# Linear attention and spectral mixing: k and v loaded in 18-row runs, and the first output tile finished whole

## The chip, the core and the metric

The kernel runs on one core of one Trainium2 chip. The metric is the device time of one execution in microseconds (us). The kernel before was timed three times: 426.86, 425.69 and 426.14 us, a median of 426.14 us. The core's engines are TensorE (PE in the profile; PEld is its weight load), VectorE (DVE), ScalarE (ACT), GpSimd (POOL) and SyncE (SP). In this kernel POOL and SP issue all transfers, which 16 DMA engines carry out.

## What is computed

A linear attention with feature map elu(x)+1 over 8 batches, 8 heads, 576 rows and 64 columns, then a spectral mix over the rows:

```python
q_p, k_p = phi(q), phi(k)
kv  = einsum('bhsd,bhse->bhde', k_p, v);  z = sum(k_p, axis=2)
x   = einsum('bhsd,bhde->bhse', q_p, kv) / (einsum('bhsd,bhd->bhs', q_p, z)[..., None] + 1e-06)
X   = rfft(x as (B, S, 512), axis=1)[:, :64]
Y   = per mode m:  X[:, m] @ (w_r[m] + 1j * w_i[m])
u   = x + irfft(Y, n=576)
out = u + maximum(u @ w_ch, 0)
```

The inputs are float32: q, k and v of 9.4 MB each, w_r and w_i of 67 MB each. The output is 9.4 MB.

## The kernel before

**Attention stage (lines 143 to 411).** For each of the 8 batches `load(b)` brings q, k and v into SBUF as 16-bit numbers; POOL issues these loads (batch 0's q comes through SP in float32). A batch is 8 heads of 576 rows, laid one after the other. For q a partition holds 18 rows in one run (`j=2 * NJ`), two runs per partition, each run covering a pair of four-head blocks; for k and v it holds 9 rows, four runs per partition. A run is one descriptor: 4,608 bytes read and 2,304 written for q, half of that for k and v. Buffers are double (`bufs=2`), so the load of batch b+2 waits until batch b's copy has been used. `exps` (ACT) and `features` (DVE) form phi of q and k; the last DVE step of `features`, line 232, copies v into the padded tile `vpad`, of which there is one, with a column of ones. `turn_q` transposes q on PE (line 242), ACT copies the result (line 249). `sum_kv` (lines 254 to 278) multiplies phi(k) by v on PE: 36 products over 64 partitions each, alternating between the lower and the upper half of the array, then two ACT copies of 64x260 into `kv`. `form_x` (five per batch) multiplies q by kv on PE (line 165) and divides on DVE (lines 296 and 299); `transform` and `place_x` are the Fourier products. All steps are pinned: each engine runs them in the order in which the program writes them. Three PSUM tiles with the tag `big` rotate among `qTp`, `kvp`, `num` and `xp`.

**Mode stage (lines 413 to 511 and 883 to 893).** Every pair of modes needs 2 MB of weights in SBUF, loaded by POOL in two halves (line 119). Five pairs are fetched ahead during the attention stage, then the channel weights `wch` and the small constant `pick_sb`; all go through the same queue, in issue order. The pair after those five (p = 5) uses the buffer of pair 0, so its loads are issued when the products of pair 0 (line 442) are done, and those come last in the attention stage's order on PE.

**Tail (lines 896 to 989).** When the last mode's weights are in, its result `Y` is transposed and multiplied by `wch` in two column halves, `zl` and `z1l` (line 924), copied into `last`, and added to each output tile through small products (line 736), rectified (ACT, lines 785 and 965), added to x (DVE, lines 969 and 809) and stored by SP. The first output tile is treated on its own (lines 910 to 952): its second column half has PSUM of its own, `z0h1`, formed from three products (lines 913, 915 and 941); PE forms `y0l` and two of these between the two halves of line 924; then each half is added (line 942), rectified (line 943) and stored (line 950), 128 KB each. The PSUM of `zl`, `z1l`, `y0l` and `z0h1` is released before `channels(2)`, the first user of the next pool (line 775). SP issues in this order: the copy of `last` to `YZ_all` (line 954), the stores of tile 0, then those of the other tiles; POOL issues the second half of the copy to `YZ_all`.

Of the kernel before, what the change touches and what calls it, by code (L numbers as in the profile page):

```python
# [10 lines left out]
F32 = mybir.dt.float32  # L11
# [3 lines left out]
ALU = mybir.AluOpType  # L15
# [28 lines left out]
def kernel(  # L44
# [97 lines left out]

    vp = sA.tile([128, NHP, NJ, 66], F16, name="vpad")
    nc.vector.memset(vp[:, :, :, 64:66], 1.0)
# [33 lines left out]
    def load(b):  # L178
        for nm, src in (("q", q), ("k", k), ("v", v)):
            rows_in = src[b].rearrange("h s d -> (h s) d").rearrange(  # L180
                "(hp r j) d -> r hp (j d)", r=128, j=2 * NJ if nm == "q" else NJ
            )
            if (nm, b) == ("q", 0):
                for c in range(2):
                    t = sA.tile([128, 2, NJ * Dh], F32, tag="x16", bufs=2, name=f"q32_{c}")
                    pin(nc.sync.dma_start(out=t, in_=rows_in[:, :, c * NJ * Dh : (c + 1) * NJ * Dh]))
                    raw[nm, b, c] = t
                pin(nc.sync.dma_start(out=id16, in_=id16_dr.ap()))
                pin(nc.sync.dma_start(out=fwd_sb, in_=fwd_dr.ap()))
                continue  # L190
            shape = [128, 2, 2 * NJ * Dh] if nm == "q" else [128, NHP, NJ * Dh]
            t = sA.tile(shape, F16, tag=f"{nm}16", bufs=2, name=f"{nm}16_{b}")
            pin(nc.gpsimd.dma_start(out=t, in_=rows_in))
            raw[nm, b] = t

    def heads(nm, b, c):
        if (nm, b) == ("q", 0):
            return raw[nm, b, c].rearrange("p o (j d) -> p o j d", d=Dh)
        if nm == "q":
            return raw[nm, b].rearrange("p o (c j d) -> p c o j d", c=2, d=Dh)[:, c]  # L200
        return raw[nm, b].rearrange("p (o c) (j d) -> p c o j d", o=2, d=Dh)[:, c]

# [51 lines left out]
    def sum_kv(b):  # L254

        kv_ps = psA.tile([128, 2, 512], F32, tag="big", bufs=3, name=f"kvp{b}")
        for hpp in range(2):
            for j in range(NJ):
                for h2 in range(2):
                    pin(  # L260
                        nc.tensor.matmul(
                            kv_ps[:, h2, hpp * 130 : hpp * 130 + 130],
                            phi["k", b][HALVES[h2], hpp, j].rearrange("p o d -> p (o d)"),
                            vp[HALVES[h2], hpp::2, j, 0:65],
                            start=(j == 0),
                            stop=(j == NJ - 1),
                        )
                    )
# [643 lines left out]
    def second_half_sums():  # L912
        pin(nc.tensor.matmul(z0, id16, e0_parts(0)[0][1][:, COLS[1]], start=True, stop=False))
        pin(
            nc.tensor.matmul(
                z0, inv2_sb[0 : 2 * NF, rows_of(0)], YZ[0][0 : 2 * NF, 1, COLS[1]],
                start=False, stop=False,
            )
        )

    for h in range(2):
# [7 lines left out]
        pin(nc.scalar.copy(out=last[:, 1, COLS[h]], in_=last_ps[h][:, 0:hw]))  # L929
        if h == 0:  # L930
            pin(nc.tensor.matmul(y0, lead_sb[0][:, rows_of(0)], last[:, 0, :]))
            second_half_sums()
    for h in range(2):
        x = x_of(0)[:, COLS[h]]
        l, r = lead_sb[0][:, rows_of(0)], last[:, 1, COLS[h]]
        if h == 0:
            z = accs[0][:, 0, COLS[0]]
            on_bank(0, {0}, nc.tensor.matmul(z, l, r, start=False, stop=True, skip_group_check=True))
        else:
            z = z0  # L940
            pin(nc.tensor.matmul(z, l, r, start=False, stop=True))
        pin(nc.vector.tensor_tensor(out=x, in0=y0[:, COLS[h]], in1=x, op=ALU.add))
        ins = nc.vector.scalar_tensor_tensor(
            out=x, in0=z, scalar=0.0, in1=x, op0=ALU.max, op1=ALU.add
        )
        if h == 0:
            on_bank(0, {0}, ins)
        else:
            pin(ins)
        nc.sync.dma_start(  # L950
            out=out_rows[0:512, COLS[h]].rearrange("(r j) d -> r j d", j=NJJ)[:, 0, :], in_=x
        )
    for h, eng in enumerate((nc.sync, nc.gpsimd)):
# [17 lines left out]

    add_inverse(0, 1, (1,))
    relu(0, 1)
# [47 lines left out]
```

## Time and profile before

The profiled execution took 426.86 us; its span from the first to the last instruction is 425.0 us, so 1.86 us lie around it.

| what | value |
|---|---|
| profiled execution / its span | 426.86 us / 425.0 us |
| median of three executions | 426.14 us |
| busy share of the span: PE, DVE, ACT, POOL | 66%, 51%, 38%, 13% |
| DMA: moved, mean rate | 93.20 MB, 219 GB/s |
| share of the chain that ended last: DMA, PE, DVE, ACT | 63%, 21%, 5%, 4% |
| k and v loads: 16 of 576 KB, median from issue to landing | 12.8 and 14.9 us |
| weight loads: 62 of 1024 KB, median from issue to landing | 12.4 and 17.0 us |

The rate counts bytes as written; loads that narrow float32 to 16 bits read twice as many. A DMA share of 1 in a stretch means that the 16 engines' packet times add up to the stretch; it can be above 1, as packets overlap on an engine.

### The profile page before, as it was taken

The numbers are of one execution on the slowest core, as the hardware profiler recorded it, in microseconds if no ns is written. First come the engines' busy times: TensorE is split into PE (matmuls) and PEld (weight loads), VectorE is DVE, ScalarE is ACT, GpSimd is POOL, SyncE is SP. The second block draws the span as 40 slices with busy tenths as digits, with TensorE's granted clock in tenths as the row PEclk, the third lists the DMA queues.
The fourth block names the chain that finished last, engine by engine and source line by source line (L and its number), as shares of the span: only waits on it lengthen the run. The fifth ranks groups of instructions, "written<-read, shape, count | busy, mean of one in ns | idle before, by whom it ended". The sixth has DMA issues, their size and how long they took to land.

```text
span 425.0 us, 7990 instructions
## 1 busy us (share of the span) xinstructions
PE 278.9 (66%) x3429; PEld 152.0 (36%) x3429; DVE 215.6 (51%) x448; ACT 161.5 (38%) x253; POOL 56.3 (13%) x99
## 2 busy tenths in 40 slices
PE   1358378878516644434344777988887698989991
PEld 0246367666302322212122333433343333455320
DVE  4599488886203453455444443443453323513893
ACT  4688487754202102000000243443443341421781
POOL 4222124210000100000000011100000000120000
PEclk9999886889955555555555597898999986999996
DMA  9999999999999999999999999999999999994796
GB/s 213 210 208 215 207 218 204 226 210 213 225 211 220 221 216 210 216 222 216 209 217 222 214 211 216 222 215 213 217 217 218 216 214 214 219 209 87 270 395 275
DMA packets 20659, 93.20 MB, mean 219 GB/s; under 512 B 2064, under 2 KB 11408, under 8 KB 16208
## 3 DMA queue, kind: packets, MB, share of 16 engines
q0 software_dynamic: 16512, 81.47, 93.5%
q1 hardware_dynamic: 4112, 11.22, 7.1%
q8 instruction: 27, 0.44, 0.4%
q14 instruction: 8, 0.07, 0.0%
HBM read 163.93 MB, written 9.44 MB: 408 GB/s over the span
## 4 chain that ended last, share of the span: by engine, by line
DMA 63%; PE 21%; DVE 5%; ACT 4%; issue 2%; POOL 2%; DVEq 0%; POOLq 0%; ACTq 0%
DMA w<-in_moe_w_i_dram 48%; DMA pick_sb<-row_pick 8%; PE P L442 8%; DMA k<-in_k_dram 7%; PE acc L736 3%; PE acc L775 2%; PE zl L425 2%; ACT ke L213 2%; POOL w L119 1%; PE eps L677 1%; ACT qT L249 1%; DVE ys L452 1%; PE z L699 1%; PE yt L460 1%; DVE x L299 1%
## 5 line engine op out<-in xcount | busy, mean ns | idle before, releaser
L442 PE MATMUL P<-w,xt_c 64*32 64x512 bf16 (+2 forms) x1000 | 50.6, 536 | 60.3 <-DMA w<-in_moe_w_i_dram 58.9
L452 DVE CAST ys<-P 128x512 f16<-128x512 f32 x32 | 22.1, 692 | 124.2 <-PE P L442 124.2
L454 ACT CAST ys<-P 128x512 f16<-128x512 f32 x31 | 18.1, 585 | 156.1 <-PE P L442 156.1
L119 POOL DMA_DIRECT2D w<-in_moe_w_r_dram x31 | 16.4, 528 | 245.7 <-PE P L442 87.5
L442 PEld LDWEIGHTS <-xt_c 64*32 64x32 bf16 (+2 forms) x1000 | 16.6, 128 | 80.2 <-DMA w<-in_moe_w_i_dram 46.8
L165 PEld LDWEIGHTS <-qT 64*128 64x128 f16 (+1 forms) x640 | 23.0, 123 | 50.1 <-issue 30.9
L677 PE MATMUL eps<-wch,xTw 128*128 128x512 f16 x144 | 40.0, 405 | 0.0
L165 PE MATMUL num<-kv,qT 64*128 64x65 f16 (+1 forms) x320 | 13.6, 209 | 25.6 <-ACT xt_c L350 12.3
L658 DVE TENSOR_TENSOR x_main<-ya,x_main 128x512 f32<-128x512 f32 x32 | 22.0, 689 | 15.2 <-PE ya L654 15.1
L660 ACT CAST x16w<-x_main 128x512 f16<-128x512 f32 x32 | 19.8, 618 | 23.5 <-DVE x_main L658 22.5
L165 PE MATMUL nw<-kv,qT 64*128 64x65 f16 (+1 forms) x320 | 19.0, 240 | 9.5 <-DVE x_tail L621 4.3
L685 ACT CAST E<-eps 128x512 f16<-128x512 f32 (+1 forms) x40 | 21.2, 539 | 8.8 <-PE eps L677 8.8
L460 PE MATMUL yt<-pick_sb,ys 128*128 128x16 f16 x252 | 11.7, 174 | 17.7 <-DMA pick_sb<-row_pick 11.0
L299 DVE TENSOR_TENSOR x<-num,rd 128x512 f16<-128x512 f32 x32 | 22.1, 692 | 1.1
L242 PE MATMUL qTp<-id,qe 128*128 128x128 f16 x144 | 15.7, 296 | 10.1 <-DVE qe L226 9.6
L213 ACT ACTIVATE qe<-q 128x1152 f16<-128x1152 f16 (+1 forms) x16 | 17.8, 1156 | 11.0 <-DMA q<-in_q_dram 6.8
L249 ACT COPY qT<-qTp 128x1152 f16<-128x1152 f16 x16 | 19.6, 1295 | 0.5 <-PE qTp L242 0.2
L213 ACT ACTIVATE ke<-k 128x1152 f16<-128x1152 f16 x16 | 17.7, 1152 | 4.8 <-DMA k<-in_k_dram 4.8
L460 PEld LDWEIGHTS <-ys 128*128 128x128 f16 x252 | 9.7, 101 | 27.6 <-DVE ys L452 14.6
L425 PE MATMUL zl<-wch,id 128*128 128x512 f16 x72 | 19.3, 404 | 0.0
L785 ACT ACTIVATE acc<-acc 128x512 f32<-128x512 f32 x34 | 18.2, 580 | 2.4 <-PE acc L736 1.5
L242 PEld LDWEIGHTS <-qe 128*128 128x128 f16 x144 | 13.5, 137 | 11.1 <-DVE qe L226 9.9
(122 smaller groups left out, 468.3 us busy)
## 6 DMA issues: line engine op xcount, KB each, us to landing
w<-in_moe_w_r_dram POOLq DMA_DIRECT2D x31, 1024.0 KB, 12.4
w<-in_moe_w_i_dram POOLq DMA_DIRECT2D x31, 1024.0 KB, 17.0
out_dram<-x_main SPq DMA_DIRECT2D x10, 512.0 KB, 3.8
k<-in_k_dram POOLq DMA_DIRECT2D x8, 576.0 KB, 12.8
v<-in_v_dram POOLq DMA_DIRECT2D x8, 576.0 KB, 14.9
q<-in_q_dram POOLq DMA_DIRECT2D x7, 576.0 KB, 12.8
out_dram<-x_main SPq DMA_DIRECT2D x2, 1024.0 KB, 5.8
q<-in_q_dram SPq DMA_DIRECT2D x2, 576.0 KB, 4.5
```

Of the source, the lines that this page charges most:

```text
L165: mm = nc.tensor.matmul(num[hpo][orow, c0 : c0 + 65], qT[rows, hpp, h2, cols], kv_sb[rows, hpp, h2, :])
L213: pin(nc.scalar.activation(out=ev[:, c], in_=heads(nm, b, c), func=AF.Exp))
L242: nc.tensor.transpose(qT_ps[:, j], phi["q", b][:, c, j].rearrange("p o d -> p (o d)"), id16,)
L249: nc.scalar.copy(out=qT[:, :, c * NJ : (c + 1) * NJ], in_=qT_ps.rearrange("p j x -> p x j"))
L299: nc.vector.tensor_tensor(out=dst.rearrange("p (o c d) -> p o c d", o=2, c=4), in0=nv[:, :, :, 0:64], in1=rden.unsqueeze(3).broadcast_to([ ...
L425: pin(nc.tensor.matmul(last_ps[0], id16, wch16[:, 0, :]))
L442: nc.tensor.matmul(P[c : c + n, :], xt_cols(dc, kk, n), w[rows, dc, :], start=(dc < NDC), stop=(dc >= n_dc - NDC), tile_position=(rows.sta ...
L452: pin(nc.vector.tensor_copy(out=st, in_=P))
L460: nc.tensor.matmul(yt_ps[:, ec, kk % 8, :], st[:, ec * 128 : ec * 128 + 128], pick_sb)
L658: pin(nc.vector.tensor_tensor(out=x, in0=acc, in1=x, op=ALU.add))
L677: nc.tensor.matmul(e_ps, xT[:, c, :], wch16[:, c, :], start=(c == 0), stop=(c == NDC - 1))
L685: pin(nc.scalar.copy(out=dst, in_=e_ps[:, cols]))
```

## The change

Two things are done. First, k and v are loaded like q, in runs of 18 rows, two per partition. Partitions 0 to 63 of a run block then hold other heads than before, each head lying in 32 partitions, so `sum_kv` forms the products in four groups of 32 partitions: two passes (`pair`), each with its own PSUM tile, 36 products and two ACT copies of 64x130 (two heads of 65 columns). Products per batch go from 36 over 64 rows to 72 over 32 rows, copies from two to four, `big` tiles by one more per batch. Second, the first output tile is no longer split: its two halves of line 924 follow each other, `y0l` comes after them, tile 0's rectified part is accumulated whole in the PSUM pair it shares with tile 1, and it is added, rectified and stored whole (256 KB). The list `QUADS`, which decides what is stored in runs of 8 KB, stands in both kernels as `(5, 6)`.

```diff
-    vp = sA.tile([128, NHP, NJ, 66], F16, name="vpad")
+    vp = sA.tile([128, 2, 2 * NJ, 66], F16, name="vpad")
...
-                "(hp r j) d -> r hp (j d)", r=128, j=2 * NJ if nm == "q" else NJ
+                "(hp r j) d -> r hp (j d)", r=128, j=2 * NJ
...
-        kv_ps = psA.tile([128, 2, 512], F32, tag="big", bufs=3, name=f"kvp{b}")
-        for hpp in range(2):
-            for j in range(NJ):
+        for pair in range(2):
+            kv_ps = psA.tile([128, 2, 512], F32, tag="big", bufs=3, name=f"kvp{b}_{pair}")
+            for j in range(2 * NJ):
                 for h2 in range(2):
+                    r0 = 64 * pair + 32 * h2
                     pin(
                         nc.tensor.matmul(
-                            kv_ps[:, h2, hpp * 130 : hpp * 130 + 130],
-                            phi["k", b][HALVES[h2], hpp, j].rearrange("p o d -> p (o d)"),
-                            vp[HALVES[h2], hpp::2, j, 0:65],
+                            kv_ps[:, h2, 0:130],
+                            phi["k", b][r0 : r0 + 32, j // NJ, j % NJ].rearrange("p o d -> p (o d)"),
+                            vp[r0 : r0 + 32, :, j, 0:65],
...
+                            tile_position=(r0, 0),
...
-        for hpo in range(2):
-            rows = HALVES[hpo]
-            pin(
-                nc.scalar.copy(
-                    out=kv_all[b][rows],
-                    in_=kv_ps[rows, :, 0:260].rearrange("p t (c o n) -> p c t o n", c=2, o=2)[
-                        :, :, :, hpo, :
-                    ],
-                )
-            )
+            for hpo in range(2):
+                rows = HALVES[hpo]
+                pin(
+                    nc.scalar.copy(
+                        out=kv_all[b][rows, pair], in_=kv_ps[rows, :, hpo * 65 : hpo * 65 + 65]
+                    )
+                )
...
-    z0 = psW.tile([128, D], F32, tag="P", bufs=2, name="z0h1")[:, COLS[1]]
...
-        if h == 0:
-            pin(nc.tensor.matmul(y0, lead_sb[0][:, rows_of(0)], last[:, 0, :]))
-            second_half_sums()
-    for h in range(2):
-        x = x_of(0)[:, COLS[h]]
...
-        nc.sync.dma_start(
-            out=out_rows[0:512, COLS[h]].rearrange("(r j) d -> r j d", j=NJJ)[:, 0, :], in_=x
-        )
+    pin(nc.tensor.matmul(y0, lead_sb[0][:, rows_of(0)], last[:, 0, :]))
+    pin(nc.vector.tensor_tensor(out=x_of(0), in0=y0, in1=x_of(0), op=ALU.add))
...
-    add_inverse(0, 1, (1,))
+    add_inverse(0, 1)
+    on_bank(
+        0, {0},
+        nc.vector.scalar_tensor_tensor(
+            out=x_of(0), in0=accs[0][:, 0], scalar=0.0, in1=x_of(0), op0=ALU.max, op1=ALU.add
+        ),
+    )
+    store(0, 1)
     relu(0, 1)
```

More of the change, by code (lines that the diff above doesn't have):

```diff
@@ L190, in load @@
                 continue
-            shape = [128, 2, 2 * NJ * Dh] if nm == "q" else [128, NHP, NJ * Dh]
-            t = sA.tile(shape, F16, tag=f"{nm}16", bufs=2, name=f"{nm}16_{b}")
+            t = sA.tile([128, 2, 2 * NJ * Dh], F16, tag=f"{nm}16", bufs=2, name=f"{nm}16_{b}")
             pin(nc.gpsimd.dma_start(out=t, in_=rows_in))
@@ L198, in heads @@
             return raw[nm, b, c].rearrange("p o (j d) -> p o j d", d=Dh)
-        if nm == "q":
-            return raw[nm, b].rearrange("p o (c j d) -> p c o j d", c=2, d=Dh)[:, c]
-        return raw[nm, b].rearrange("p (o c) (j d) -> p c o j d", o=2, d=Dh)[:, c]
+        return raw[nm, b].rearrange("p o (c j d) -> p c o j d", c=2, d=Dh)[:, c]
     def flat(nm, b):
@@ L254, in sum_kv @@
     def sum_kv(b):
[L256 to L258 removed]
+        for pair in range(2):
+            kv_ps = psA.tile([128, 2, 512], F32, tag="big", bufs=3, name=f"kvp{b}_{pair}")
+            for j in range(2 * NJ):
                 for h2 in range(2):
+                    r0 = 64 * pair + 32 * h2
                     pin(
                         nc.tensor.matmul(
[L262 to L264 removed]
+                            kv_ps[:, h2, 0:130],
+                            phi["k", b][r0 : r0 + 32, j // NJ, j % NJ].rearrange("p o d -> p (o d)"),
+                            vp[r0 : r0 + 32, :, j, 0:65],
                             start=(j == 0),
[L266 to L276 removed]
+                            stop=(j == 2 * NJ - 1),
+                            tile_position=(r0, 0),
+                        )
+                    )
+            for hpo in range(2):
[4 more added lines that the diff above has]
+                    )
                 )
[L278 removed]
     def form_x(b, jj):
@@ L909 @@
     pin(nc.vector.tensor_copy(out=last[:, 0, COLS[1]], in_=y_ps[1].rearrange("p c r -> p (c r)")))
-    z0 = psW.tile([128, D], F32, tag="P", bufs=2, name="z0h1")[:, COLS[1]]
[L912 to L917, printed above, removed]
-            )
-        )
     for h in range(2):
@@ L929 @@
         pin(nc.scalar.copy(out=last[:, 1, COLS[h]], in_=last_ps[h][:, 0:hw]))
-        if h == 0:
-            pin(nc.tensor.matmul(y0, lead_sb[0][:, rows_of(0)], last[:, 0, :]))
-            second_half_sums()
-    for h in range(2):
-        x = x_of(0)[:, COLS[h]]
[L935 to L949, printed above, removed]
-        nc.sync.dma_start(
-            out=out_rows[0:512, COLS[h]].rearrange("(r j) d -> r j d", j=NJJ)[:, 0, :], in_=x
-        )
+    pin(nc.tensor.matmul(y0, lead_sb[0][:, rows_of(0)], last[:, 0, :]))
+    pin(nc.vector.tensor_tensor(out=x_of(0), in0=y0, in1=x_of(0), op=ALU.add))
     for h, eng in enumerate((nc.sync, nc.gpsimd)):
```

## The prediction

> **What bounds the kernel now.** I read the chain of waits first, then the rate and DMA share of stretches, then the order of single instructions where the change touches it. The chain of waits (start, length, what):
>
> ```profile
> 33.47 15.89 DMA k<-in_k_dram
> ...
> 71.94 20.44 DMA w<-in_moe_w_i_dram
> 92.66 32.88 DMA pick_sb<-row_pick
> ...
> 362.68 17.84 DMA w<-in_moe_w_i_dram
> 380.56 1.84 PE P L442 x27
> ...
> 416.63 1.13 DVEq L1016
> ```
>
> One DMA wait hands over to the next from 33 to 380 us: the time is what the queue of loads takes, as long as it never runs dry. The first and the last load of that queue are fixed, so a byte that is moved faster anywhere in it is a gain at the end. After 380.56 a chain of short PE and DVE steps follows, and then the stores. The second view is the table of stretches (stretch, length, PE, PEld, DVE, ACT, POOL busy, granted clock, DMA share, GB/s). Which load is in flight I took from the issue order of the queue and the lengths of the loads; the first two stretches hold k and v only, the next two mostly q, the last weights only:
>
> ```profile
> 45.60:50.20 4.60, 0.31 (x4) 0.21 (x2) 1.61 (x5) 2.97 (x3) 0.00 (x0) 0.95 1.21 208
> 67.80:72.00 4.20, 3.55 (x74) 3.04 (x68) 3.38 (x8) 3.59 (x6) 2.76 (x5) 0.72 1.20 206
> ...
> 51.30:53.20 1.90, 0.88 (x12) 0.63 (x11) 0.38 (x2) 0.94 (x2) 0.00 (x0) 0.50 1.12 213
> 73.40:75.00 1.60, 0.19 (x2) 0.16 (x2) 1.39 (x3) 1.58 (x3) 0.70 (x2) 1.00 1.12 214
> 280.00:320.00 40.00, 32.00 (x303) 14.57 (x301) 16.71 (x32) 16.61 (x31) 4.23 (x8) 0.96 1.01 216
> ```
>
> In none of them is the DMA share below 1: the engines are full already in the attention stage, and k and v run at 206 to 208 GB/s while q, in runs twice as long, has 213 and 214.
>
> **Part 1, the loads.** 16 loads of 576 KB (589,824 bytes) are 9.44 MB. At 207 GB/s they take 45.6 us, at q's 213 GB/s 44.3 us: 1.3 us less. Bounds: another q stretch of the trace, straight behind a weight load, has only 206 GB/s (no gain), and at the weights' 216 against 206 it would be 2.1 us. I take 1.3, as most q stretches lie at 212 to 216 and the k and v stretches at 206 to 208. POOL's issues stay as many, and q with half the descriptors takes about as long to issue (0.70 us at 40.93) as k and v (0.77 and 0.75 us after it), so nothing changes there. The gain reaches the end: PE waited 2.04 us for the weights at 380.56, more than 1.3, and the pieces of the last pair stand behind the same queue.
>
> [...]
>
> **Part 1, the products.** What PE does for one batch at full and at half clock, and the issue that waits for the end of the stage:
>
> ```profile
> 40.50 1.22 PE L261 MATMUL kvp<-vpad,ke 64*128 64x130 f16 x36 [0.78 <-ACT qT L249]
> ...
> 78.45 2.11 PE L261 MATMUL kvp<-vpad,ke 64*128 64x130 f16 x36
> ...
> 113.47 1.10 PE L442 MATMUL P<-w,xt_c 64*32 64x512 bf16 x32 [1.40 <-ACT xt_c L350]
> ...
> 114.92 0.52 POOL L119 DMA_DIRECT2D w<-in_moe_w_r_dram  x1 [21.72 <-PE P L442]
> ```
>
> 36 products of 130 columns take 1.22 us, 34 ns each (2.11 us, 59 ns, in stretches where the granted clock is 0.50 to 0.72): two of them overlap, as one alone is recorded with 214 to 312 ns. After the change 72 products alternate in the same way between two row groups, so I take the same pace: one more block of 1.22 to 2.13 us per batch. Behind it stand, on ACT, the copies to `kv` (two of 0.37 us now; four after, of which only the last two trail: 0.27 us each by the slope between 128x256 at 0.37 and 128x512 at 0.58), and on DVE the copy to `vpad`, which waits until PE has read the old one; both hold `form_x`, and all of the stage after it.
>
> The five blocks after 49.4 us (there ACT waits for k anyway, idle 4.07 and 0.63 us, which covers batches 0 to 2) take 1.33, 2.13, 2.11, 1.53 and 1.22 us: 8.3 us more at the very most. DVE is idle 0.24, 0.39 and 0.16 us before `form_x`, the copies give 0.2 us back each, and in the last batch ACT, not PE, is the later one (3.83 us of DVE's idle time). That leaves about 1.0, 1.7, 1.7, 1.1 and 0.3; as some stretches will also find PE less idle and the clock higher, I take 4.5 us, between 0 and 8.3. [...] The rows agree on two speeds (2.11 against 1.22 us). [...]
>
> What hides it: pair 0's products end at 114.6 and release the load of pair 5, issued at 114.92, while the queue holds work until `pick_sb` lands at 92.66 + 32.88 = 125.5. A load issued into an idle queue needs about 2.7 us before its bytes flow (the second copy to `YZ_all` takes 3.9 us to land, 256 KB at 210 GB/s are 1.2 of it), and the queue will now end 1.3 us earlier and about 1 us before the landing is seen: the issue may come as late as 120.5. Slack 5.6 us, delay 4.5: hidden, cost 0. If the cover is gone, every further us is a us of idle DMA and of time. The later issue (pair 6, 128.19) waits for pair 1, which waits for `pick_sb`, not for this stage. The loads of batch 7 wait for `features(5)`: q's issue at 67.69, its turn in the queue at 72.5 at the earliest (v of batch 6 before it), less 2.7 is 2 us of slack, against a delay of about 1 there, as only batch 3 with its 1.0 precedes it.
>
> **Part 2, the first tile.**
>
> ```profile
> 393.31 0.61 PE L924 MATMUL z1l<-wch,Y 128*128 128x256 f16 x4
> ...
> 393.95 0.37 ACT L929 CAST last<-z1l 128x256 f16<-128x256 f32 x1 [0.86 <-PE z1l L924]
> ...
> 394.38 0.27 PE L941 MATMUL z0h<-last,lead_sb 128*128 128x256 f16 x1 [0.35 <-ACT last L929]
> ...
> 394.92 0.42 DVE L943 SCALAR_TENSOR_TENSOR x_main<-z0h,x_main 128x256 f32<-128x256 f32 x1
> ...
> 395.40 0.59 PE L775 MATMUL acc<-E,id 128*128 128x512 f16 x2
> ...
> 396.25 0.69 DVE L969 TENSOR_TENSOR x_main<-acc,x_main 128x512 f32<-128x512 f32 x1 [0.90 <-PE acc L736]
> ```
>
> The second half of line 924 starts only at 393.31, behind `y0l` and two sums, though `Y` was ready at 391.8; and `channels(2)` (395.40) starts when the last reader of that pool's PSUM, line 943, ends at 395.34. After: the second four products follow the first four (start 392.08, 0.11 us each) at 392.5 and end by 393.1; ACT's second copy runs 393.15 to 393.5 (now 393.95 to 394.32), so `last` is ready 0.8 us earlier. `y0l` ends at 393.4; DVE adds it and rectifies in two steps of 0.69 (128x512, line 969) until 394.8. PE forms four products of line 736 from 393.55 to 394.5, then `channels(2)`, with nothing to wait for but DVE's first step (394.1), until 395.1, then one product; DVE's line 969 starts at 395.4 instead of 396.25. SP: the copy to `YZ_all` goes out at 393.6 (now 394.35), tile 0's single store at 394.85 (now 395.03 and 395.60; one issue less, of the 1.70 us that the two take), the next store 0.85 earlier; POOL's copy moves likewise, which line 736 for later batches needs. From 396.25 to 417.8 DVE's steps follow each other almost without idle time, and the DMA share is 1.01 and 0.98 from 400 to 420, so the end moves with the start. I take 0.8 us of gain; at best 1.0 (all PE work between the halves), at worst a loss of 0.5 (2 x 0.69 less 2 x 0.42, if only DVE's longer steps counted).
>
> **Sum.** Span 425.0 - 1.3 - 0.8 = 422.9, plus the 1.86 around it 424.8 for the profiled execution of 426.86; against the median, 0.72 lower, 424.0.
>
> **Rivals.** (a) Only the tail's gain arrives: run length is not what makes k and v slower (the 206 GB/s of the q stretch at 42.9), or a late pair-5 load eats about as much. 426.14 - 0.8 = 425.3, within 0.3% of before. For it: the rates differ by 3% only. Against it: five of six q stretches are above every k and v stretch. (b) The other side: products over 32 rows push pair 5's load out. If PE stays at half clock, or overlaps the 32-row products less well than the 64-row ones, the five blocks grow by 2.1 us or more each, 10 us in all; the issue then comes at about 125 against 120.5, 4.5 us of empty queue: 424.0 + 4.5 = 428.5. It costs from an issue after 120.5 on, and makes the kernel slower than before by 0.3% from 124 on. For it: PE's share of time at half clock from 48 to 80 us, and blocks that no row of 32 rows shows. Against it: pace and overlap of the 64-row products. (c) The split's first store was worth something: then the tail loses 0.5 instead of 0.8 gained, 424.0 + 1.3 = 425.3, no change again.
>
> **How the numbers follow.** Forecast 0.58, its own range 423.0 (gains of 2.1 and 1.0) to 424.8; (a) and (c) 0.25 together; (b) 0.17. A change of 0.3%, 1.3 us, is about what a measurement here can tell from none. Faster 0.58, same 0.25, slower 0.17. The range goes from 422.6 (the largest gains and the spread of half a us between executions) to 427.0, which leaves out the worse half of (b).
>
> **What would show it.** In the changed kernel's profile: k and v stretches near 213 GB/s; 72 products in 2.4 to 4.3 us; pair 5's load issued between 117 and 121 and the DMA share still 1 around 125; PE's wait for the last full pair starting some 1.3 us earlier than 380.56; line 969's first step 2 us earlier than 396.25. It is wrong if the DMA share drops near 125, or if k and v keep 207 GB/s.

## The result, and the profile after

| | kernel before | changed kernel |
|---|---|---|
| median | 425.91 us (425.42 to 426.86, 4 runs) | 422.61 us (422.50 to 422.93, 4 runs) |
| profiled execution / its span | 426.86 / 425.0 us | 422.50 / 420.7 us |
| products recorded on PE | 3429 | 3714 |
| packets of the loads' queue, for the same 81.47 MB | 16512 | 12416 |

The ratio is 0.9921 with a 95% interval of 0.9902 to 0.994: 3.3 us faster, where 424.0 was forecast, 2.1 below the 426.14 of the three executions known then (a fourth, of 425.42, makes the median 425.91).

The chain of waits of the changed kernel, as before (start, length, what):

```profile
91.66 33.05 DMA pick_sb<-row_pick
...
362.86 26.11 DMA w<-in_moe_w_i_dram x2
391.35 1.02 PE acc L732 x4
...
413.57 1.13 DVEq L987
```

The DMA wait now reaches to 388.97 in one piece: the products of the last full pair (line 442, now 438) are no longer a link of their own. The last link of the chain, on DVE, starts 3.06 us earlier (413.57 against 416.63).

The table of stretches for the changed kernel (stretch, length, PE, PEld, DVE, ACT, POOL busy, clock, DMA share, GB/s); k, v and q now have runs of one length:

```profile
45.60:50.20 4.60, 4.40 (x64) 3.10 (x63) 3.81 (x8) 3.78 (x5) 1.65 (x3) 1.00 1.11 212
67.80:72.00 4.20, 3.32 (x44) 2.24 (x45) 4.06 (x11) 3.65 (x4) 2.77 (x5) 0.88 1.11 212
73.40:75.00 1.60, 1.60 (x16) 1.60 (x16) 1.56 (x4) 1.17 (x3) 0.54 (x1) 0.50 1.10 210
280.00:320.00 40.00, 31.86 (x309) 14.81 (x317) 16.70 (x32) 16.10 (x30) 4.35 (x8) 0.96 1.02 216
```

The two stretches that ran at 206 and 208 GB/s run at 212. Then the order of single instructions: products, the issue that waits for the stage, the last full pair, and the first tile.

```profile
75.39 3.63 PE L259 MATMUL kvp<-vpad,ke 32*128 32x130 f16 x72
88.22 2.06 PE L259 MATMUL kvp<-vpad,ke 32*128 32x130 f16 x72
...
114.51 0.52 POOL L119 DMA_DIRECT2D w<-in_moe_w_r_dram  x1 [22.31 <-PE P L438]
...
379.16 1.11 PE L438 MATMUL P<-w,xt_c 64*32 64x512 bf16 x32 [0.49 <-DMA w<-in_moe_w_i_dram]
...
389.34 0.23 DVE L507 CAST Y<-y_last 128x64 f16<-128x64 f32 x1 [1.47 <-PE y_last L501]
...
390.93 0.37 ACT L914 CAST last<-z1l 128x256 f16<-128x256 f32 x1
391.14 0.69 DVE L916 TENSOR_TENSOR x_main<-y0l,x_main 128x512 f32<-128x512 f32 x1 [0.80 <-PE y0l L915]
391.95 0.69 DVE L939 SCALAR_TENSOR_TENSOR x_main<-acc,x_main 128x512 f32<-128x512 f32 x1
392.21 0.60 PE L771 MATMUL acc<-E,id 128*128 128x512 f16 x2
393.07 1.34 DVE L933 TENSOR_TENSOR x_main<-acc,x_main 128x512 f32<-128x512 f32 x2 [0.44 <-PE acc L732]
```

Pair 5's load goes out at 114.51, 0.41 us earlier than before in spite of 36 more products a batch. The last full pair waits 0.49 instead of 2.04 us for its weights. From the start of the copy to `Y` to the first whole-tile addition (line 969, now 933) it is 3.73 us; before it was 4.69 (391.56 to 396.25).

### The profile page after: what moved, and what is told of

It is laid out like the page before. It is cut to its first block, busy times and chain, and to the rows that moved or that the text cites. A ratio compares the mean times of both kernels' runs of the same rounds, so it can differ in the third digit from the quotient of the medians.

```text
span 420.7 us, 8570 instructions
## 1 busy us (share of the span) xinstructions
PE 292.1 (69%) x3714; PEld 162.7 (39%) x3714; DVE 215.7 (51%) x446; ACT 163.5 (39%) x269; POOL 56.9 (14%) x99
## 3 DMA queue, kind: packets, MB, share of 16 engines
q0 software_dynamic: 12416, 81.47, 93.1%
## 4 chain that ended last, share of the span: by engine, by line
DMA 64%; PE 22%; DVE 6%; issue 2%; POOL 2%; ACT 2%; DVEq 0%; POOLq 0%; ACTq 0%
DMA w<-in_moe_w_i_dram 51%; DMA pick_sb<-row_pick 8%; PE P L438 7%; DMA k<-in_k_dram 5%; PE acc L732 3%; PE acc L771 2%; PE kvp L259 2%; POOL w L119 2%; PE zl L421 1%; PE eps L673 1%; ACT ke L210 1%; DVE ys L448 1%; DVE x L295 1%; PE ya L650 1%; PE yt L456 1%
## 5 line engine op out<-in xcount | busy, mean ns | idle before, releaser
L450 ACT CAST ys<-P 128x512 f16<-128x512 f32 x31 | 18.1, 585 | 155.6 <-PE P L438 155.6
L119 POOL DMA_DIRECT2D w<-in_moe_w_r_dram x31 | 17.3, 557 | 247.4 <-PE P L438 97.4
L259 PE MATMUL kvp<-vpad,ke 32*128 32x130 f16 x576 | 24.3, 261 | 9.0 <-ACT qT L246 6.1
L259 PEld LDWEIGHTS <-ke 32*128 32x128 f16 x576 | 22.2, 115 | 10.7 <-issue 8.2
L239 PE MATMUL qTp<-id,qe 128*128 128x128 f16 x144 | 14.1, 277 | 11.3 <-DVE qe L223 9.4
L165 PE MATMUL num<-kv,qT 64*128 64x65 f16 (+1 forms) x320 | 16.4, 218 | 5.5 <-DVE x L295 3.2
## 6 DMA issues: line engine op xcount, KB each, us to landing
w<-in_moe_w_i_dram POOLq DMA_DIRECT2D x31, 1024.0 KB, 17.4
q<-in_q_dram POOLq DMA_DIRECT2D x7, 576.0 KB, 12.7
```

Source lines behind the costliest of these rows:

```text
L119: nc.gpsimd.dma_start(out=w_in[p][half::2], in_=two.rearrange("g (r dc) e -> (g r) dc e", dc=NDW))
L165: mm = nc.tensor.matmul(num[hpo][orow, c0 : c0 + 65], qT[rows, hpp, h2, cols], kv_sb[rows, hpp, h2, :])
L259: nc.tensor.matmul(kv_ps[:, h2, 0:130], phi["k", b][r0 : r0 + 32, j // NJ, j % NJ].rearrange("p o d -> p (o d)"), vp[r0 : r0 + 32, :, j, 0 ...
```

## The experiments

The kernel before was timed again beside the others, on five chips. Its 82 executions lie in two groups: 31 between 425.12 and 425.79 us, 51 between 426.04 and 427.05 us, and none between. The groups are about 1 us apart, as much as the terms that are to be measured, so groups are given beside medians. A ratio is that to the kernel before, timed beside the version in question.

**e1, the first part alone.** Lines 143 to 278 as changed, lines 910 to 972 as before.

> The kernel before with the first part alone (k and v in 18-row runs, 72 products a batch); first tile in halves as before. Theory: the gain of the changed kernel (3.3 us) has three terms, and this kernel gets two: the queue of loads ends 0.7 us earlier (the small weight pieces of the last pair were read 0.7 us earlier in the changed kernel), and, as the last full pair's weights come earlier after PE's keep-warm products, the clock stays up in that pair's products, up to 1.5 us more. So 423.7 to 425.2, with PE's wait ahead of the last full pair's products below 1 us and the granted clock near 1 there. Rival 1, the loads give everything: 422.6, as the changed kernel. Rival 2, the tail gives everything: 425.9. Rival 3, the clock at the last pair is chance: 425.2 (-0.7), whatever the clock there.

Measured: 424.77 us (423.54 to 425.56, 12 runs), ratio 0.9966 (0.9953 to 0.998); the kernel before had 426.04 beside it, so 1.27 us less. Neither part gives all: rivals 1 and 2 are out. In its profile the last full pair has no wait and full clock, and yet there is a half-clock stretch, later. Stretches from 388 us on:

```profile
388.00:390.00 2.00, 1.63 (x36) 1.34 (x34) 0.23 (x1) 0.00 (x0) 0.00 (x0) 0.91 0.05 8
390.00:392.00 2.00, 2.00 (x10) 0.92 (x7) 0.71 (x2) 0.75 (x2) 0.00 (x0) 0.50 0.00 0
392.00:394.00 2.00, 1.70 (x9) 1.07 (x9) 0.75 (x3) 0.37 (x1) 0.24 (x1) 0.74 0.00 0
```

The clock column is a mean over the stretch: 0.91 in the first means that the half clock began at 389.64, 0.74 in the third that it ended at 393.04, 3.4 us later. It lies in the first tile's chain here. So the half clock is no property of the last full pair's wait alone, and "the loads part brings the clock back" is not the whole story.

**e2, the second part alone.** Lines 910 to 972 as changed, the rest as before.

> The kernel before with the second part alone: the first tile whole, its store whole, k and v as before. Theory: the chain from Y to the first whole-tile addition becomes 0.96 us shorter (4.69 to 3.73 us), the end moves by as much: 424.9 to 425.1, and PE's wait for the last full pair's weights and the half clock behind it stay as before (about 2 us of wait, some 1.9 us for the 32 products). Rival 1, the loads give everything: 425.9. Rival 2, the tail gives everything: 422.6. Rival: losing the split's first store costs something at the end: 425.9 or more.

Measured: 425.08 us (424.02 to 425.64, 12 runs), ratio 0.9979 (0.9968 to 0.9991), 0.96 us below before. From `Y` (390.06) to line 937 (393.80) it is 3.74 us, as in the changed kernel. The half clock did not come in this profile, and there was no wait for the last full pair: the expectation missed that. (The profiled execution, 424.02 us, is the fastest of the twelve.) By the medians the two parts make 2.2 us together, and the change makes 3.3. The fastest executions add up: 425.12 before, 423.54 with the first part, 424.02 with the second and 422.42 with both (of 82, 12, 12 and 15), so 1.58 and 1.10 against 2.70. What the medians have beyond that is how often an execution falls into an upper group.

**e3 and e4, keep-warm products.**

```diff
-    FILL = {**{p: 5 for p in range(18, 27)}, 27: 8, 28: 2, 29: 7, 30: 7}
+    FILL = {**{p: 5 for p in range(18, 27)}, 27: 8, 28: 2, 29: 7, 30: 12}
```

> The kernel before with 12 instead of 7 keep-warm products ahead of the last full pair; nothing else. They write a spare tile and no output depends on them. Five more of 0.21 us shorten PE's wait for the weights from 2.04 to about 1 us. Theory: the clock then stays at full in the last full pair, its 32 products take 1.1 instead of 1.9 us, the products behind it (0.6 us of 1.7) as well, and the time falls by 0.7 to 1.5 us: 424.4 to 425.2. Rival: the clock there is chance, or the pieces of the last pair set the end anyway: 425.9, no change.

> The changed kernel with 1 instead of 7 keep-warm products ahead of the last full pair; nothing else. PE then waits some 1.75 us for the weights in place of 0.49. Theory: the clock falls for the last full pair as it did in the kernel before, and 0.7 to 1.5 us of the 3.3 are lost: 423.3 to 424.1. Rival, the clock is no part of the gain: 422.6, as the changed kernel.

Measured: e3 426.58 us (425.50 to 427.98, 12 runs), half a us above before; e4 423.43 us (422.26 to 424.76, 6 runs). The lines above are e3's; e4 sets `30: 1` in the changed kernel. Both edits changed another place than was meant: the products of entry 30 come behind the last full pair, not ahead of it. e3 still waits 1.99 us there and its five products stand in PE's way behind it; e4 lets PE idle 0.89 us ahead of `y_last` and has a half-clock stretch from 389.1 to 392.5. They say nothing about the wait at 380, but e4 shows again where a second such stretch can fall.

**e5, the changed kernel in more executions.**

> The changed kernel once more, unchanged, in more executions. The 29 executions of the kernel before lie in two groups (425.2 to 425.5, and 426.0 to 426.9), and the profiles show half-clock stretches of PE after 380 us in some executions (before at 381 to 385, the loads alone at 389 to 393) and none in others (the tail alone, the changed kernel). New theory: one such stretch costs about 1.3 us and falls by chance; the two parts give 1.3 to 1.6 and 1.0 to 1.2 us in either group, and the four executions at 422.5 to 422.9 were all of the lower group. So the changed kernel has an upper group too, at 423.7 to 424.5, and its median over a dozen executions lies between 422.6 and 423.7. Rival: the changed kernel is free of the half-clock stretch: all executions at 422.4 to 423.0, median 422.6.

Measured: 423.03 us (422.42, 422.58, 422.80, 423.25, 423.88, 423.94), ratio 0.9929 (0.9913 to 0.9946). There is an upper group, but a thin one: with e17 and the first four, 12 of 15 executions are at 422.42 to 422.98.

**e6, two keep-warm products in the waits around `y_last`.**

```diff
+            if dc == NDL - 1:
+                keep_warm(1)
...
         nc.vector.tensor_copy(out=Y8[:, :, NL - 1, :], in_=y_last)
+        keep_warm(1)
```

> The changed kernel with one keep-warm product of 0.21 to 0.38 us in the wait of the last products (y_last) for the last weight piece, and one in the 0.32 us wait behind them for DVE's copy. They write a spare tile. Theory of the half-clock stretch: they make PE's idle part from 388 to 390 us smaller, so fewer executions have the half clock in the first tile's chain: median 422.4 to 422.9, upper group thinner. Rival: the two products only lie in PE's queue: +0.1 to +0.3 us, same two groups as the changed kernel.

Measured: 423.56 us (422.67 to 425.07, 6 runs). PE is busy 1.90 instead of 1.64 us (e5) between 388 and 390, the chain behind is not later, and three of six executions are in the upper group all the same. No gain.

**e7, short runs again in the changed kernel.**

```diff
-            pin(nc.gpsimd.dma_start(out=t, in_=rows_in))
+            for part in (slice(None),) if nm == "q" else (slice(0, NJ * Dh), slice(NJ * Dh, None)):
+                pin(nc.gpsimd.dma_start(out=t[:, :, part], in_=rows_in[:, :, part]))
```

> The changed kernel with each load of k and v issued as two DMAs of 9-row runs (2,304 B read, 1,152 B written each), the tiles as in the changed kernel: 32 more issues on POOL, the products unchanged. Theory: the run length is what the loads part gains by, so k and v stretches go back to 206 to 208 GB/s and 0.7 to 1.5 us are lost: 423.3 to 424.2. Rival: the length does not matter, the gain of the loads part comes from the order of the products and the slots they turn over: 422.6 to 423, as the changed kernel. If the 32 further issues (about 0.75 us each on POOL) delayed the loads, k and v stretches would show a DMA share below 1.

Measured: 424.00 us (423.66 to 424.94, 6 runs), 0.97 us above e5, timed beside it. The two stretches of k and v:

```profile
45.60:50.20 4.60, 4.60 (x63) 3.28 (x59) 3.84 (x9) 3.60 (x4) 1.65 (x3) 1.00 1.20 203
67.80:72.00 4.20, 3.60 (x52) 2.67 (x53) 4.06 (x10) 3.30 (x4) 1.76 (x4) 0.77 1.21 206
```

The products are those of the changed kernel, the runs are short, and the rates are back at 203 and 206 with the DMA share above 1; 81 MB are in at 387.3 instead of 386.1 us (e5). The loads also come in twice as many issues here, but the kernel before, with short runs and the usual issues, has the same rates. The length of the runs is what the loads gain by; the order of the products is not.

**e8, every block of products twice.**

```diff
+            for _ in range(2):
+                for j in range(2 * NJ):
```

> The changed kernel with every block of products of sum_kv done twice, into the same PSUM group from its start: 144 products a batch, same output. It makes the delay of the attention stage that the prediction feared: 2.1 to 3.7 us more PE work per batch, 8 to 20 us over the stage. Theory (the cover is the queue's work until pick_sb lands at 124.7): the issue of pair 5's load moves from 114.5 to 124 or later; beyond about 119.7 each us of delay is an empty queue, so the DMA share falls below 0.5 for some us between 120 and 130 and the time is 3 to 15 us above the changed kernel's. Rival: PE hides the products again (its work is in the shadow of the loads until batch 6): issue before 119.7, time unchanged within 0.5 us.

Measured: 434.28 us (433.73 to 434.30 in three executions, 442.69 in one). Pair 5's issue, and the stretches around it:

```profile
131.89 0.52 POOL L119 DMA_DIRECT2D w<-in_moe_w_r_dram  x1 [37.53 <-PE P L439]
```

```profile
124.00:126.00 2.00, 2.00 (x28) 1.35 (x23) 0.37 (x1) 0.00 (x0) 0.00 (x0) 0.70 0.38 62
126.00:128.00 2.00, 1.05 (x13) 0.76 (x14) 0.32 (x1) 1.36 (x3) 0.00 (x0) 1.00 0.00 0
128.00:130.00 2.00, 1.04 (x22) 0.86 (x18) 0.92 (x2) 0.20 (x1) 0.00 (x0) 1.00 0.00 0
130.00:132.00 2.00, 1.11 (x32) 0.57 (x31) 0.37 (x2) 0.71 (x2) 0.11 (x1) 1.00 0.23 74
```

The queue is empty for some 7 us, as rival (b) described, and weakly filled around that: 24 MB are in 1.9 us later than in the changed kernel, and from 132 to 138 us the rates are 123 and 184 GB/s. The time is 11.6 us above the changed kernel's 422.68, the issue 17.4 us later: 11.6 us before 131.89 is 120.3, the point up to which the delay was free. By the bytes, which come 11.5 us (40 MB, 206.7 instead of 195.2) to 11.0 us later (81 MB, 397.0 instead of 386.0), it is 120.4 to 120.9. The prediction had put it at 120.5.

**e9, keep-warm products ahead of the last full pair** in the kernel before, this time in the right place (`29: 12`).

> The kernel before with 12 instead of 7 keep-warm products between the pair before the last full pair and the last full pair, where its profile has PE waiting 2.04 us for weights and the half clock from 380.8 on (the earlier try lengthened the group behind the last full pair, which is another place). Theory: the wait falls to about 1 us, the clock stays at full from 380 to 385, the upper of the two groups of executions (426.0 to 426.9) is gone or thinner: median 425.1 to 425.7. Rival: the half clock is not caused by that wait, two groups as before, median 426.0 to 426.5.

Measured: 425.64 us (12 runs; before 426.37 beside it), ratio 0.9993 (0.9981 to 1.0005), so no sure gain as a whole. But ten of the twelve lie at 425.34 to 425.86, the lower group, and two at 427.2 and 427.4. In its profile the wait and the half clock at 380 are gone.

**e10 and e11, the kernel before, profiled twice more.**

> One more profile of the kernel before, unchanged. Theory: if its time lies in the lower group (425.1 to 425.5) the profile shows full clock from 380 to 395 us; if it lies in the upper one (426.0 to 426.9) there is a half-clock stretch of 3.4 us, at 381 or at 390. Rival: time and half-clock stretch have nothing to do with each other.

> As the look before it: one more profile of the kernel before, to be sorted by the same rule.

Measured: 426.42 and 425.54 us, one of each group. Stretches of e10:

```profile
378.00:380.00 2.00, 0.67 (x4) 0.10 (x1) 0.00 (x0) 0.00 (x0) 0.00 (x0) 1.00 1.04 217
...
382.00:384.00 2.00, 2.00 (x16) 0.96 (x14) 0.92 (x2) 0.53 (x1) 0.00 (x0) 0.50 1.01 209
384.00:386.00 2.00, 2.00 (x22) 1.27 (x21) 0.42 (x1) 0.59 (x1) 0.00 (x0) 0.66 0.94 181
```

and of e11:

```profile
378.00:380.00 2.00, 2.00 (x19) 0.80 (x23) 0.00 (x0) 0.58 (x1) 0.00 (x0) 1.00 1.00 209
...
382.00:384.00 2.00, 2.00 (x26) 1.22 (x23) 0.43 (x2) 0.58 (x1) 0.00 (x0) 1.00 0.97 199
384.00:386.00 2.00, 2.00 (x13) 0.70 (x15) 0.00 (x0) 0.00 (x0) 0.00 (x0) 1.00 0.99 192
```

e10 waits 2.02 us at 378.7 and has the half clock from 382 to 385.4; e11 has neither, and its time is 0.88 us less. The rule stated before the two profiles holds in both, and in the first profile of the kernel before (426.86 us, half clock from 380.8 to 384.2): the upper group is the one with the half-clock stretch. With this, e11 is the execution that the changed kernel has to be held against, not the one that was predicted from. Three profiles and e9 are the evidence; the next experiment has a profile that does not fit.

**e12, the first tile's last step and store split again.**

```diff
-    on_bank(
-        0, {0},
-        nc.vector.scalar_tensor_tensor(
-            out=x_of(0), in0=accs[0][:, 0], scalar=0.0, in1=x_of(0), op0=ALU.max, op1=ALU.add
-        ),
-    )
-    store(0, 1)
+    for h in range(2):
+        x = x_of(0)[:, COLS[h]]
+        on_bank(
+            0, {0},
+            nc.vector.scalar_tensor_tensor(
+                out=x, in0=accs[0][:, 0, COLS[h]], scalar=0.0, in1=x, op0=ALU.max, op1=ALU.add
+            ),
+        )
+        nc.sync.dma_start(
+            out=out_rows[0:512, COLS[h]].rearrange("(r j) d -> r j d", j=NJJ)[:, 0, :], in_=x
+        )
```

> The changed kernel with the first tile's last step (rectify and add) and its store in two column halves, the first half's store going out 0.25 us earlier, with 1,024-byte runs; all products and channels stay as in the changed kernel. Theory: the tail's gain is the order of the products and the freed PSUM, not the store; the stores that follow fill the DMA queues anyway, and DVE takes 0.84 in place of 0.69 us: 0 to +0.3 us against the changed kernel (422.4 to 423.9 in its two groups). Rival, the split's first store was worth something: 0.3 us or more faster than the changed kernel.

Measured: 423.04 us (422.92, 422.98, 423.04, 423.15, 424.08): its lower group is 0.3 to 0.4 us above the changed kernel's. Rival (c) is out: the split gains nothing, and the time is longer; where the 0.4 us lie, the table below shows. The profiled execution is the longest of the five (424.08), and it has the full clock from 376 to 396 us, with a half-clock stretch earlier, from 366.4 to 373.2. So an execution can lie high without the stretch behind 380 us.

**e13 to e16, where PE's code is loaded.** In e11 and the changed kernel the last store is issued at 416.63 and 414.73, and the span ends 7.14 and 5.97 us later. The same bytes are stored, so something else at the end differs. The queues' view (queue, packets, MB, share) for e11 from 412 to 416 us:

```profile
q1 hardware_dynamic: 217, 1.65, 101.3%
q8 instruction: 1, 0.02, 1.4%
```

Beside the stores (q1) there is one packet of 16 KB of program code (q8), which takes 0.88 us. The changed kernel has it from 404 to 408 us:

```profile
q1 hardware_dynamic: 562, 1.56, 101.1%
q8 instruction: 1, 0.02, 1.6%
```

The number of these packets goes with PE's instructions: 27 before, for 3429 products and as many weight loads recorded, 254 instructions each; 29 for 3714 and as many with 36 more products a batch, 256 each; 33 in e8. So the place of the last one can be moved by products that do nothing:

```diff
+        if p == 0:
+            spare = [psW.tile([128, D], F32, tag="P", bufs=2, name=f"spare{i}") for i in range(2)]
+            for i in range(42):
+                pin(nc.tensor.matmul(spare[i % 2][:, 0:16], id16, id16[:, 0:16]))
         work_slot(p, "mid")
```

> The changed kernel with 84 tiny products (16 columns, into a spare tile that nothing reads) put on PE while it waits for pick_sb after pair 0 (115 to 124.7 us, where PE is idle); the output is the same. Each is two instructions, so the 16 KB blocks in which PE's code is loaded (256 instructions, about 24 us of the tail) begin 168 instructions sooner: the last block, loaded at 405.7 us in the changed kernel, should come at about 390 and 414. In the kernel before it comes at 413 to 415. Theory of the code block: one DMA engine spends 0.9 us on it, late in the stores, and is the last to finish: the time from the last store's issue to the end grows from 6.0 us (414.73 to 420.7) to about 6.7 (as in the kernel before, 417.79 to 425.0: 7.2; second look of before 416.63 to 423.8: 7.2; tail alone 415.53 to 422.2: 6.7), time +0.4 to +0.9: groups at 423.0 to 423.5 and 424.3 to 424.8. Rival: what ends the stores later in the kernels without the loads part is something else: unchanged, 422.4 to 423.9.

> The control to the run before: 42 tiny products in the same place, 84 instructions; the last code block should come at about 398 and the next one only after the end. Theory of the code block: no straggler, time as the changed kernel (422.4 to 423.9, median about 422.7) or up to 0.3 us less. Rival, the added products themselves cost time (they delay pair 1, or shift PE's clock): half of what the 84 cost.

> The tail part alone (k and v as in the kernel before) with the 42 tiny products: the last code block should move from 413.4 to about 405. Theory of the code block: the end after the last store's issue shortens from 6.7 to about 6.0 us, as in the changed kernel, and the time falls by 0.4 to 0.9 us below the tail alone (median 425.1): 424.2 to 424.7. Rival: no change, 425.1.

> The kernel before with the 42 tiny products and nothing else: last code block from 414 to 415 to about 406. Theory of the code block: 0.4 to 0.9 us faster than before: 425.3 to 425.8 for a median of 426.2, groups near 424.7 and 425.9; and the split tile's pieces go on as before. Rival: no change.

| kernel | median us | first tile's store | last code packet, us before the end | last store's issue to the end of the last DMA packet, us | from there to the end of the span, us |
|---|---|---|---|---|---|
| before, e10, e11 | 426.33 (82 runs) | split | 9.9, 10.5, 9.3 | 5.48, 5.34, 5.39 | 1.70, 1.74, 1.75 |
| e3, e9 (before, more keep-warm) | 426.58, 425.64 | split | 11.9, 11.8 | 5.64, 5.56 | 1.69, 1.70 |
| e16, before + 42 | 425.01 | split | 18.1 | 4.66 | 1.68 |
| e1, loads alone | 424.77 | split | 16.7 | 4.61 | 1.68 |
| e12, changed, split | 423.04 | split | 15.5 | 4.71 | 1.69 |
| e2, tail alone | 425.08 | whole | 8.8 | 5.43 | 1.28 |
| e15, tail alone + 42 | 423.47 | whole | 17.6 | 4.57 | 1.27 |
| changed, e5, e17 | 422.68 (15 runs) | whole | 15.0 each | 4.73, 4.61, 4.87 | 1.24, 1.25, 1.25 |
| e4, e6, e7 | 423.43, 423.56, 424.00 | whole | 13.7, 15.5, 15.1 | 5.08, 4.84, 4.81 | 1.25, 1.26, 1.25 |
| e14, e18, changed + 42 | 422.13, 422.16 | whole | 22.9, 22.7 | 4.31, 4.36 | 1.25, 1.24 |
| e8, products twice | 434.28 | whole | 28.3 | 3.90 | 1.25 |
| e13, changed + 84 | 422.07 | whole | 30.3 | 3.97 | 1.23 |

The fifth column follows the place of the code packet, with the split store as with the whole one: 5.3 to 5.6 us with the packet 9 to 12 us before the end, 4.6 to 4.9 at 15 to 18, 4.3 at 23, 3.9 to 4.0 at 28 to 30. The rate at the very end shows what the time goes into (GB/s in slices of 0.2 us; e11 from 416 us, the changed kernel and e13 from 413 us):

```profile
GB/s 451 287 328 451 389 389 410 389 318 420 358 420 379 379 389 461 399 410 430 399 369 358 41 41 20 20 41 20 20 20 0 0 0 0 0 0 0 0 0 0
...
GB/s 328 614 287 410 532 164 614 246 410 369 451 389 389 369 318 440 348 379 440 317 379 512 420 389 461 389 348 164 21 41 20 20 0 0 0 0 0 0 0 0
...
GB/s 532 205 573 410 287 614 287 410 266 389 430 389 430 389 348 348 430 369 399 369 369 471 400 451 389 410 369 430 21 0 0 0 0 0 0 0 0 0 0 0
```

In e11 the last 1.5 us or so move 20 to 41 GB/s, where 16 engines together moved some 400: the DMA share from 421 to 422 us is 0.06, the time of one engine in 16. In the changed kernel that lasts 0.8 us, in e13 0.2 us at most. One engine that finishes late is what the theory of the code block said; that it is the engine which had carried the code packet is not shown, as the trace does not name the engine.

The last column follows the first tile's store: 1.68 to 1.75 us split, 1.23 to 1.28 us whole, whatever the place of the code packet. It lies behind the last DMA packet, so no store is delayed there. SP's waits from 410 us on (waiting line, what for: us in total, times, longest us), for e11 and then for the changed kernel:

```profile
SPq L1016 <- DMA out_dram<-x_main: 5.1, 1, 5.1
...
SPq L987 <- DMA out_dram<-x_main: 2.9, 3, 1.2
SPq L987 <- DMA out_dram<-x_tail: 1.2, 1, 1.2
```

At the program's end SP waits for the stores' eight semaphores one after the other, in the same order in both kernels, and about 0.06 us apart where nothing holds them (in the first profile of before the eight waits end from 423.65 to 424.08 us). The stores use them in turn, so one store more moves the last store to another of them. In e11 it has the first of the order: SP waits once, for 5.1 us, and then runs through the other seven behind the last landing. In the changed kernel it has the last: the seven are done, the seventh at 418.56 us, when it lands (the eighth ends at 419.79). So the 0.4 to 0.5 us go with the number of stores, not with what the split store does to the transfers; a whole tile with another number of stores was not run.

e15 and e16 moved the packet as expected and fell by more than expected in the medians: 1.6 below e2, which was timed on another chip, and 1.4 below the kernel before. From packet to packet the fifth column gives 0.9 (e2 to e15) and 0.7 to 0.8 us (the kernel before to e16); the profiled execution of e16 is 0.5 below e11, and neither has a wait for the last full pair. The rest of the medians' fall is in the groups: e16's eleven executions lie at 424.57 to 425.63 us without a gap. e14, meant as a control, was expected at 0 to 0.3 us below the changed kernel and lies 0.55 below: a packet at 15 us still costs. e13 missed its aim: no packet came at 414, the last one was at 389.8, so it became a second case without a late packet, and is the fastest. That a packet put back to 414 in the changed kernel would cost what it cost before was therefore not shown in that direction; e2 against e15 and e11 against e16 show it in the other.

**e17 and e18, the changed kernel and the version with 42 spare products, timed side by side.**

> The changed kernel beside the version with the 42 tiny products, on the same chip in the same call. Theory of the code block and of the half clock: as in its ten executions so far, two groups, 422.4 to 422.9 and 423.2 to 424, median 422.6 to 423.1.

> The changed kernel with the 42 tiny products once more, beside the changed kernel itself. Theory: no code block behind 398 us, so the stores end 0.4 to 0.6 us sooner, and, if the half-clock stretch stays away as in its five executions so far, no upper group: median 422.0 to 422.3, 0.4 to 0.8 us below the changed kernel of the same call. Rival: the 0.6 us between the calls were the chip's or the day's: both the same within 0.2 us.

Measured: 422.68 us (422.51 to 422.98) and 422.16 us (422.05 to 422.52); against before 0.9916 (0.9902 to 0.993) and 0.9905 (0.9889 to 0.9921). From 399 to 421 us e18's queues carry stores only:

```profile
## 3 DMA queue, kind: packets, MB, share of 16 engines
q1 hardware_dynamic: 2114, 7.80, 88.7%
```

None of e17's five executions is in the upper group, where two groups were expected. The last store is issued at 414.77 in e17 and 414.67 in e18, the spans end at 420.9 and 420.3: the half us lies behind the last issue. This version, products that compute nothing, beats both kernels.

## Why the prediction was right in direction and small in size

Held against e11 (425.54, no half clock), the changed kernel's profile splits its 3.1 us of span like this: the copy to `Y` starts 1.07 us earlier (390.41 to 389.34), the first tile's chain is 0.95 shorter (4.68 to 3.73), DVE's steps from there to the last are 0.1 longer, and the end behind the last store's issue is 1.17 shorter.

**Loads, forecast 1.3.** The mechanism is right (e7): 212 instead of 206 to 208 GB/s. The size was too large. The packets show the bytes 0.8 to 0.9 us earlier than in e11 (the first 24 MB were in at 120.2 instead of 121.1 us, 78 MB at 371.8 instead of 372.7, 81 MB at 386.0 instead of 386.8). At `Y`, between profiles with the full clock behind 380 us, it is 0.72 (e2 against the changed kernel), 0.85 (e15 against e14) and 1.07 us (e11), inside the bounds of 0 to 2.1. e7, with the products of the changed kernel, lost 0.97 us by runs of 1,152 written bytes.

**Products, forecast 4.5 us of delay, hidden.** The five blocks took 2.31, 2.37, 3.63, 2.06 and 2.37 us, 12.7 in all against 8.3 before: PE's extra work was 4.4 us, but the delay was -0.4. What took it: PE's waits ahead of line 165 for ACT's `xt_c` fell from 12.3 to 0.4 us (the sum over the waits by releaser), so PE filled time in which it had waited. That an extra `big` tile per batch moves which step gets which PSUM slot is a likely reason, but was not tried by itself. So the forecast size of the delay failed, without a cost in time. What a later issue would have cost was as forecast: the free slack ended at 120.3 to 120.9 (e8), forecast 120.5.

**First tile, forecast 0.8.** The chain gave 0.95; the steps came as described (`last` by 391.3, `channels(2)` right behind the four products at 392.21, line 933 at 393.07). Rival (c) fell with e12.

**The step that failed** is the end of part 2, "the end moves with the start", and with it the sum: 1.17 us of the 3.1 arose behind the last store's issue, a term that the sum put at nothing. 0.66 of them lie in the draining of the stores (5.39 to 4.73 us). That is PE's code: 288 more products moved its last 16 KB from 414.5 us, among the last stores, to 405.7 us, and e2 against e15, with nothing changed but spare products, gives 0.86. The other 0.51 (1.75 to 1.24) lie behind the last DMA packet, in SP's closing waits: the prediction had counted the whole store as an issue less, and not that this decides which semaphore comes last. No row in the prediction told of the packet's place, but the queues' part of the page lists the code packets, and part 1 doubles the products. Where the stores drain, the last packet's place was worth 0.7 to 0.9 us between 9 to 10 and 15 to 18 us before the end, and 1.4 us to 30. What it costs while the loads run, no run here separates.

**The base of the sum** was the second weak point. It was an upper-group execution (426.86) with a half-clock stretch from 380.8 to 384.2, and the 0.72 us to the median were taken off as if every execution moved alike. In three profiles of the kernel before the group goes with the stretch, and e9, which shortened the wait, has ten of twelve executions in the lower group; e12's profile, the longest of its five without the stretch, shows that it is not the only cause. That the changed kernel falls into its upper group in 3 of 15 executions, against 51 of 82 before, adds to the medians' difference. Why it does so more rarely is in part argued: at 380 it waits 0.49 instead of 2.04 us; for the stretch at 389 (e1, e4), e6 found no cure.

Of the rivals, (a) and (c) named no change and did not come; (b)'s mechanism exists and its price is real (e8), its condition was not met.

## What to carry to other kernels

Before a small change is costed, sort the executions of the kernel: two groups a us apart mean that the profiled one has to be placed first, and the sum made against its like. Look for what else shares the DMA engines at the very end, the code packets among them: here products added on PE 300 us earlier moved them, with 0.52 us of the time (e17 against e18), and a change of that size may be nothing else. Look also behind the last DMA packet: one store more or less moved the end by 0.4 us there, with no transfer in flight. Here a delay ahead of an issue cost nothing up to the moment when the queue would have run dry (an issue at 120.3 instead of 114.51 us), and doubling the suspected work showed where that is.

## What was not expected of the hardware

- The granted clock fell to half for 3.4 us (389.64 to 393.04 in e1, 382 to 385.4 in e10, 380.80 to 384.21, 3.41 us, in the first profile of before), after a wait of only 2.0 us in two of them. Of the 3.41 us ahead of the fall PE had been busy for 1.37 (first profile of before), 1.39 (e10), 2.48 (e4) and even 3.08 us (e1). In e1 they end in 16-column products (`y_last`). e11 was busy for 3.00 us from 386.6 to 390.0 and kept the full clock, so what decides is open.
- Products over 32 rows, alternating between two row groups, run at 29 to 33 ns each at full clock (2.06 to 2.37 us for 72) and 50 ns at half clock (3.63 us at 75.39): no slower than those over 64 rows (34 and 59 ns).
- A 16 KB packet of code took 0.88 to 1.06 us (the 27 and 29 of the two kernels' profiles), and the end of the stores went with the place of the last one. From the last store's issue to the last packet's end it is 5.3 to 5.6 us with the code packet 9 to 12 us before the end, 4.6 to 4.9 at 15 to 18, 4.3 at 23 and 3.9 to 4.0 at 28 to 30.
- The closing waits of SP took 0.4 to 0.5 us longer behind the last DMA packet when one more store had been issued (1.68 to 1.75 against 1.23 to 1.28 us).
